# K, V and the gate logit in the spare columns of the last FFN chunk, and one written list of steps for the whole main phase

## The chip, the cores and the metric

The kernel runs on one core of a Trainium2 chip. The metric is device microseconds of that core, from the first to the last instruction and what lies around them; the median of the runs counts.

## The reference, cut to what matters

```python
B, S, D, H = 1, 2048, 512, 32          # Dh = 16; one K and one V head for all 32 query heads
q = x @ wq ; k = x @ wk ; v = x @ wv   # k and v are 2048 x 16
a = softmax(q k^T / 4) v, heads side by side, @ wo
b = (gelu(x @ w_gate) * (x @ w_up)) @ w_down      # F = 1376, tanh form of gelu
g = sigmoid(sum(x * gate_w))
out = g * a + (1 - g) * b
```

Everything is float32. The kernel makes most products in three passes: each factor is split into a high part (its rounded value, hi) and a low part (the rest, lo), and hi·hi, hi·lo and lo·hi are added in PSUM.

## The kernel before, in words

The 2048 tokens are four groups of 512 (TG). The 1376 hidden columns of the FFN are eleven chunks of 128 (NF), so that the last chunk has 1376 − 10·128 = 96 real columns and 32 of zeros.

**Prologue** (lines 291 to 322). The groups come in the order 1, 2, 3, 0. For each, TensorE (PE) makes `pk`, 12 products of 128x512 that give K (three times), V and the gate logit from a small weight tile `wkv` (L296), and then four blocks of Q, `pq`, of 12 products each (L301). `post_k` copies K into `kp` and V into `vt`; `post_q` splits a block of Q, takes its largest value for the softmax bound and writes it to DRAM (`scr`), from where it is read back in another layout as `Q`. Beside this ScalarE (ACT) and VectorE (DVE) split the next group of x. Behind the last block stand the 24 products of FFN chunk 0 of group 0 at full width (L509 to L518), with the bound's small steps `pairmax` and `shift_row` among them; then a branch on the bound (L528), of which the normal data take the short side.

**Main phase** (L564 on). Three kinds of work share PE, and a word of letters says how they are laced:

- S or Z: one score step, two products of 51 rows at once (L584), into one of three PSUM tiles of two banks: S takes tile 0 or 1 in turn, Z takes tile 2. ACT follows with one exponential of 128x1024 (L587). There are 1024 such steps.
- V: probabilities times V for one key chunk, four products onto four column strips (L657), in plain float32, which the trace shows as eight rows. There are 512 of them, 16 to a unit; behind a unit `norm` copies the sum out of PSUM, and the next unit uses the same bank. Here a run of V steps with other work ahead and behind is called a visit.
- F: a pair of products on the upper and the lower 64 rows of PE (L364), one for `z` and one for `y`, between H (the job's two PSUM banks are taken; z lies in tile 2) and R (the results go on to DVE). A gate job (an FFN chunk's gate and up product) and an output job (attention result times wo) have 24 pairs, a down job 18 or 12.

Behind a gate job's R, DVE copies z out (L389) and makes the gelu's inside (L392, L393), ACT the tanh, DVE the rest (L399, L400) and the two halves `hh` and `hl`. Weights arrive through `st` and are split by DVE (hi, L129) and GpSimd (lo, L130) in slots of the jobs. `WORDS` holds one word per kind of job (twelve for FFN and output jobs, one for the end). A V asks for a count, and `visit` (L667) decides how many steps are taken: never past a unit's end, at most four, the rest carried to the next visit. Output jobs come in as soon as a group's attention is ready.

**Tail**: norm of the last unit and the last output product.

Of the kernel before, what the change touches and what calls it, by code (L numbers as in the profile page):

```python
# [19 lines left out]
P = 128  # L20
# [12 lines left out]
QK = 51  # L33
SCALE = DH ** -0.5
# [7 lines left out]
WORDS = {  # L42
# [13 lines left out]
}  # L56
# [3 lines left out]
def mix_kernel(ctx, tc, xT, wq, wkv, wo, wf, out):  # L60
# [17 lines left out]
    shs = dr.tile([NTG * NB, 2, 3, 4, TG], F32, name="shs")  # L78

# [29 lines left out]
    wks = pp.tile([P, NC, P], F32, name="wks")  # L109
    wqs = p2.tile([P, NC, D], F32, tag="xr", name="wqs", bufs=4)  # L110
    xr = {tg: p2.tile([P, NC, TG], F32, tag="xr", name=f"xr{tg}", bufs=4) for tg in order[:3]}
    nc.scalar.dma_start(wks, wkv)
# [9 lines left out]
    load_x(order[1])  # L122
    load_x(order[2])
# [8 lines left out]
    wkh = pp.tile([P, NC, P], F32R, name="wkh")  # L132
    wkl = pp.tile([P, NC, P], F32R, name="wkl")
# [18 lines left out]
    split(nc.vector, nc.vector, wkh, wkl, wks)  # L152
    split_x(order[0], 0)
    split_x(order[0], 1)
    split_x(order[0], 2)
    split_x(order[0], 3)
# [27 lines left out]
    def post_k(tg, pk):  # L184
        sl = slice(tg * TG, (tg + 1) * TG)
        for r in (0, 64):
            nc.scalar.copy(kp[r : r + KR, sl], pk[0:KR])
        nc.scalar.copy(vt[32 * tg : 32 * tg + 32], pk[64:96])
        nc.vector.tensor_reduce(kmx[0:KR, tg : tg + 1], pk[0:KR], axis=AX, op=ALU.max, apply_absolute_value=True)
        for r in (32, 96):  # L190
            nc.vector.tensor_sub(kp[r : r + 16, sl], pk[32:48], kp[r : r + 16, sl])

    def post_v():
        pv = ps_a.tile([P, 4, P], F32, tag="pa", name="pv")
# [25 lines left out]
    chunks = [(tg, f) for tg in range(NTG) for f in range(NF)]  # L220
    W = {}
    stage = {}
# [6 lines left out]
    def fetch_w(n):  # L229
        if n < len(chunks):  # L230
            stage[n] = cp.tile([P, 3, D], F32, tag="st", name=f"st{n}", bufs=2)
            nc.sync.dma_start(stage[n], wf[chunks[n][1]].rearrange("p (t d) -> p t d", t=3))

    def split_w(n):
        if n not in stage:
            return []
        st = stage.pop(n)
        gh = cp.tile([P, 2, NC, P], F32R, tag="gh", name=f"gh{n}", bufs=2)
        gl = cp.tile([P, 2, NC, P], F32R, tag="gl", name=f"gl{n}", bufs=2)
        dh = cp.tile([P, D], F32R, tag="dh", name=f"dh{n}", bufs=4)  # L240
        dl = cp.tile([P, D], F32R, tag="dl", name=f"dl{n}", bufs=4)
        W[n] = gh, gl, dh, dl
        view = lambda t: st[:, t].rearrange("p (c f) -> p c f", c=NC)
        parts = [(gh[:, t], gl[:, t], view(t)) for t in range(2)] + [(dh, dl, st[:, 2])]
        return [lambda part=part: split(nc.vector, nc.gpsimd, *part) for part in parts]
# [45 lines left out]
    fetch_w(0)  # L291
    fetch_w(1)
    for ti, tg in enumerate(order):
        xh, xl = xs[tg]
        pk = ps_a.tile([P, TG], F32, tag="pa", name=f"pk{tg}")
        passes(pk, lambda c: wkh[:, c], lambda c: wkl[:, c], lambda c: xh[:, c], lambda c: xl[:, c], NC)  # L296
        post_k(tg, pk)
        for b in range(NB):
# [3 lines left out]
            if ti + 1 < NTG:  # L302
                split_x(order[ti + 1], b)
            post_q(tg, b, pq, ti == NTG - 1 and b == NB - 1)
            if ti == NTG - 1 and b == 0:
                for part in split_w(0):
                    part()
            if ti == NTG - 1 and b == 1:
                post_v()
            if ti == NTG - 1 and b == 2:  # L310
                load_q(0)
# [21 lines left out]
    wo_jobs = []  # L333
    hold = []
# [50 lines left out]
    def gelu(n, g, u):  # L385
# [16 lines left out]
        def halves():  # L402
            hh = cp.tile([P, TG], F32R, tag="hh", name=f"hh{n}", bufs=3)
            hl = cp.tile([P, TG], F32R, tag="hl", name=f"hl{n}", bufs=3)
# [12 lines left out]

    def gate_job(n):
        tg, f = chunks[n]

        def begin():
            flush(todo)
            if n == 1:
                fetch_w(2)
            fetch_w(n + 2)
            if n == 2:
                fetch_split("wo", wo, lambda: (woh, wol), lazy)
            defer(5 if n == 1 else 2, lambda: todo.extend(split_w(n + 1)))
            return weights_terms(n, 0), weights_terms(n, 1)

        def end(z, y):
# [4 lines left out]
            if f == NF - 1 and tg + 1 < NTG:  # L436
                reload_x(tg + 1)

        kind = "ABC"[f % 3] if f < NF - 2 else "ab"[f - NF + 2]
        return "L" if n == 1 else kind, begin, end  # L440

    def down_job(batch, i):
        tg, f = chunks[batch[0][0]]
# [6 lines left out]
        def begin():  # L450
            if f == 0 and i == 0:
# [3 lines left out]
        def end(z, y):  # L455
            for k, ps in ((i, z), (i + 1, y)):
                o = acc[tg][:, k]
                w = gc[:, 4 * tg + k : 4 * tg + k + 1]
                if f == 0:
# [4 lines left out]
        return ("DE" if len(batch) == 3 else "de")[i // 2], begin, end  # L464
# [10 lines left out]
    def wo_job(g, i):  # L475
        def begin():
            flush(lazy)
            return [[t for bl in range(NB) for t in wo_terms(g, k, bl)] for k in (i, i + 1)]
# [5 lines left out]
        return "WX"[i // 2], begin, end  # L484

    def jobs():
        for n, (tg, f) in enumerate(chunks):
            if n > 0:
                yield gate_job(n)
            if f % 3 == 2 or f == NF - 1:  # L490
                flush(chain)
                batch = hold[:]
                hold.clear()
                for i in (0, 2):
                    yield down_job(batch, i)
            while wo_jobs and wo_jobs[0][0] <= now[0]:
                g = wo_jobs.pop(0)[1]
                for i in (0, 2):
                    yield wo_job(g, i)
# [9 lines left out]
    ps = ps_f.tile([P, TG], F32, tag="pf", name="g0")  # L509
    terms = weights_terms(0, 0)  # L510
    chain_mm(ps, terms[:9], last=False)
    pairmax()
    chain_mm(ps, terms[9:], first=False)
    up0 = ps_a.tile([P, TG], F32, tag="pa", name="u0")
    terms = weights_terms(0, 1)
    chain_mm(up0, terms[:3], last=False)
    shift_row()
    chain_mm(up0, terms[3:], first=False)  # L518
    gelu(0, ps, lambda: up0)
    rest = split_w(1)  # L520
    for part in rest[:2]:
        part()
# [67 lines left out]
    def norm(u):  # L590
# [34 lines left out]
        def high(cs):  # L625
            if (g, b) not in O:
                assert not [j for j in wo_jobs if j[1] < g]
# [3 lines left out]
        def low(cs):  # L631
            oh, ol = O[g, b]
            nc.vector.tensor_sub(ol[:, cs], N[:, cs], oh[:, cs])  # L633
            if g < NTG - 1 and b == NB - 1:
                wo_jobs.append((now[0] + 4, g))
# [25 lines left out]
    at_s, at_v, carry = [0], [0], [0]  # L661
# [5 lines left out]
    def visit(k):  # L667
        if at_v[0] == nsteps:
            return
# [5 lines left out]
        if left - take == 1 and take < 3 and ready > take:  # L675
            take += 1
        carry[0] = want - take
        for _ in range(take):
            pv(at_v[0])
            at_v[0] += 1  # L680
        if take and at_v[0] % NKC == 0:
            if at_v[0] < nsteps:
                norm(at_v[0] // NKC - 1)

    def play(word, job=None):
        if job:
            X, Y = job[1]()
        for t in word.split():
# [14 lines left out]
            else:  # L703
                assert next(pairs, None) is None
                job[2](z, y)
# [6 lines left out]
    rest[2]()  # L712
# [4 lines left out]
    for job in jobs():  # L717
        play(WORDS[job[0]], job)
    while at_v[0] < nsteps:
        play(WORDS["T"])  # L720
# [16 lines left out]
_INS = ["xT", "wq", "wkv", "wo", "wf"]  # L737


def _layout(i):  # L740
# [7 lines left out]
    part = lambda w: w.reshape(NC, P, -1).transpose(1, 0, 2)  # L748
    pad = np.zeros((P, NC, 16), np.float32)
    wk = part(f("A_wk"))  # L750
    ins["wkv"] = np.concatenate([wk, wk, wk, pad, part(f("A_wv")), part(f("gate_w")), pad[:, :, 0:15], pad, pad], axis=2)
    ins["wo"] = f("A_wo").reshape(NB, 2, 4, DH, D).transpose(2, 1, 3, 0, 4).reshape(P, NB, D)

    def cols(w):
        w = np.pad(w, ((0, 0), (0, NF * P - F)))
# [3 lines left out]
    ins["wf"] = np.concatenate([cols(f("B_w_gate")), cols(f("B_w_up")), wd], axis=2)  # L759
# [18 lines left out]
```

## Time and profile before

| | |
|---|---|
| median of 3 runs | 1265.14 us (1263.65 to 1265.22) |
| the profiled execution | 1263.97 us |
| its span, first to last instruction | 1262.2 us |
| PE busy in the span | 1247.7 us |
| ACT busy | 1031.1 us |
| DVE busy | 574.8 us |
| first product of the prologue, first score step, last V step | 6.27, 72.80, 1245.0 us |

All times of single instructions are of the profiled execution, in which PE ran at a mean granted clock of 0.997. Products overlap on PE, so a row's own duration is longer than the time until the next one starts; what a product costs is read from the distance between starts.

### The profile page before, as it was taken

The page shows a single profiled execution, that of the slowest core. Times are in us where ns is not written, and L with a number is a line of the kernel's source. Part 1 is how long each engine was busy: PE and PEld are TensorE (multiplying, and loading weights), DVE is VectorE, ACT ScalarE, POOL GpSimd, SP SyncE. Part 2 cuts the span into 40 slices and gives each one's busy share as a digit, 9 for nine tenths or more (in the row PEclk, how much of TensorE's full clock was granted, in tenths as well). Part 3 has the DMA queues.
Part 4 walks back from the last instruction along what each step waited for, and adds up shares of the span by engine and source line. Part 5 has one row for each costly group of instructions (what it writes and reads, how often), then busy time and mean ns, then how long its engine had stood idle before and what let it go on. Part 6 is the DMA issues. An engine that isn't in the chain of part 4 may idle for free.

```text
span 1262.2 us, 23911 instructions
## 1 busy us (share of the span) xinstructions
PE 1247.7 (99%) x9886; PEld 667.8 (53%) x9886; DVE 574.8 (46%) x861; ACT 1031.1 (82%) x1118; POOL 222.6 (18%) x264
## 2 busy tenths in 40 slices
PE   9989999999999999999999999999999999999998
PEld 6855544554455555554555555554554555555554
DVE  6773352625553163443555145362546325354334
ACT  5358888888888888888888888888888888888883
POOL 3132211211220120212131012120232002112100
PEclk9999999999999999999999999999999999999999
DMA  8441111111210211111020021011111003101000
GB/s 316 166 155 56 44 39 47 39 39 56 81 40 14 70 54 39 64 40 56 28 93 1 31 81 64 26 53 39 51 53 59 15 31 106 39 27 39 14 1 35
DMA packets 26305, 72.63 MB, mean 58 GB/s; under 512 B 3984, under 2 KB 3984, under 8 KB 26192
## 3 DMA queue, kind: packets, MB, share of 16 engines
q1 hardware_dynamic: 25792, 70.01, 16.3%
q8 instruction: 79, 1.29, 0.4%
q0 software_dynamic: 256, 0.79, 0.2%
q14 instruction: 34, 0.28, 0.1%
q10 hardware_dynamic: 144, 0.26, 0.1%
HBM read 57.67 MB, written 13.37 MB: 56 GB/s over the span
## 4 chain that ended last, share of the span: by engine, by line
PE 90%; DVE 1%; ACT 1%; POOL 0%; issue 0%; DMA 0%; SPq 0%; ACTq 0%; DVEq 0%; POOLq 0%
PE acc L657 37%; PE s L584 22%; PE z L364 16%; PE y L364 14%; ACT p L587 1%; PE wos L349 1%; POOL gl L130 0%; DMA st<-wf 0%; DVE acc L472 0%; PE wof L349 0%; DVE sq L393 0%; DVE ol L633 0%; SPq L284 0%; DVE oh L629 0%; DVE dh L129 0%
## 5 line engine op out<-in xcount | busy, mean ns | idle before, releaser
L587 ACT ACTIVATE p<-s 128x1024 f32<-128x1024 f32 x1024 | 979.9, 1025 | 172.7 <-PE s L584 166.5
L657 PE MATMUL acc<-p,v 128*32 128x512 f32 x4096 | 490.9, 598 | 0.0
L584 PE MATMUL s<-Q,kp 51*128 51x512 f32 x2048 | 391.3, 419 | 5.2 <-SPq L528 2.7
L584 PEld LDWEIGHTS s<-Q,kp 51*128 51x128 f32 x2048 | 186.4, 184 | 247.4 <-ACT p L587 170.2
L657 PEld LDWEIGHTS acc<-p,v 128*32 128x32 f32 x4096 | 107.8, 109 | 247.0 <-issue 241.8
L130 POOL TENSOR_TENSOR gl<-st,gh 128x512 fp32r<-128x512 f32 x88 | 124.0, 1429 | 399.8 <-PE s L584 176.6
L389 DVE COPY gs<-z 128x512 f32<-128x512 f32 x43 | 29.7, 691 | 246.0 <-PE z L364 142.6
L364 PE MATMUL y<-xh,gh 64*128 64x512 f32 x344 | 138.6, 403 | 1.5 <-DVE gs L400 1.5
L364 PE MATMUL z<-xh,gh 64*128 64x512 f32 x344 | 138.4, 402 | 0.6 <-POOL mark L372 0.4
L364 PE MATMUL z<-xl,gh 64*128 64x512 f32 x344 | 134.9, 392 | 0.0
L364 PE MATMUL y<-xl,gh 64*128 64x512 f32 x344 | 134.9, 392 | 0.0
L364 PE MATMUL y<-xh,gl 64*128 64x512 f32 x344 | 134.8, 392 | 0.0
L364 PE MATMUL z<-xh,gl 64*128 64x512 f32 x344 | 134.8, 392 | 0.0
L372 POOL MEMSET mark<- 1x1 f32 x81 | 8.7, 108 | 583.3 <-PE y L364 579.2
L462 DVE SCALAR_TENSOR_TENSOR acc<-z,gc,acc 128x512 f32<-128x512 f32 x24 | 18.0, 751 | 146.8 <-PE z L364 125.1
L364 PEld LDWEIGHTS z<-xh,gh 64*128 64x128 f32 x344 | 64.3, 187 | 16.9 <-POOL mark L372 8.9
L364 PEld LDWEIGHTS z<-xh,gl 64*128 64x128 f32 x344 | 63.8, 186 | 9.7
L364 PE MATMUL z<-dh,hl 64*128 64x512 f32 x176 | 68.9, 391 | 0.0
L364 PE MATMUL y<-dh,hl 64*128 64x512 f32 x176 | 68.8, 391 | 0.0
L364 PE MATMUL z<-dh,hh 64*128 64x512 f32 x176 | 68.8, 391 | 0.0
L364 PE MATMUL z<-dl,hh 64*128 64x512 f32 x176 | 68.7, 390 | 0.0
L364 PE MATMUL y<-dh,hh 64*128 64x512 f32 x176 | 68.7, 390 | 0.0
(152 smaller groups left out, 1581.4 us busy)
## 6 DMA issues: line engine op xcount, KB each, us to landing
st<-wf SPq DMA_DIRECT2D x44, 768.0 KB
scr<-q SPq DMA_DIRECT2D x16, 512.0 KB
Q<-scr SPq DMA_DIRECT2D x64, 128.0 KB
Q<-scr SPq DMA_DIRECT2D x64, 64.0 KB
out<-acc SPq DMA_DIRECT2D x16, 256.0 KB
xr<-xT SPq DMA_DIRECT2D x6, 512.0 KB
xst<-xT SPq DMA_DIRECT2D x12, 256.0 KB
xr<-xT SPq DMA_DIRECT2D x4, 256.0 KB
```

The lines of the kernel that those rows point to most:

```text
L130: eng_l.tensor_sub(lo, src, hi)
L349: nc.tensor.matmul(ps, a, b, start=(first and q == 0), stop=(last and q == len(terms) - 1), skip_group_check=True)
L364: mm = nc.tensor.matmul(ps, a[rs], b[rs], start=(half == 0 and q == 0), stop=(half == 1 and q == len(X) - 1), skip_group_check=True)
L372: relay = nc.gpsimd.memset(mark, 0.0).ins
L389: nc.vector.tensor_copy(gs, g)
L462: nc.vector.scalar_tensor_tensor(o, ps, w, o, op0=ALU.mult, op1=ALU.add)
L584: nc.tensor.matmul(ps[:, j * TG : (j + 1) * TG], kp[rs, kc * P : (kc + 1) * P], Q[u][rs, pr], start=True, stop=True)
L587: nc.scalar.activation(p, ps, AF.Exp, bias=0.0, scale=SCALE)
L657: nc.tensor.matmul(accp[u][32 * j : 32 * j + 32], vt[:, kc], pb[s, j // 2][:, (j % 2) * TG : (j % 2 + 1) * TG], start=(kc == 0), stop=(kc ...
```

## The change

**Columns.** The separate weight tile for K, V and the logit is gone. In the last FFN chunk, K's 16 columns stand twice behind the 96 gate columns, and V's 16 and the logit's one behind the 96 up columns. The two products of this chunk, `gf` and `uf` (12 of 128x512 each), are made in the prologue for all four groups, in the place of `pk`. Rows 96 to 127 of them are K and V; rows 0 to 95 go through gelu in the prologue (`first_gelu`), on ACT, DVE and GpSimd, and the resulting halves of groups 1 to 3 are written to DRAM (`hs`) and read back when the group's turn comes (`reload_h`). So chunk 0 of each group in the new numbering (r = 0) is the last FFN chunk, and has no gate job. The next chunk's gate and up products of group 0 are the 24 full-width products in front of the branch. The splits of its weights and of the one after it move into the prologue's groups.

**List.** In place of words and `visit`'s rules there is a list of 78 words, one for each job in order (`f` FFN, `w` output, `t` the end). A V's count is taken as it stands.

```diff
-        pk = ps_a.tile([P, TG], F32, tag="pa", name=f"pk{tg}")
-        passes(pk, lambda c: wkh[:, c], lambda c: wkl[:, c], lambda c: xh[:, c], lambda c: xl[:, c], NC)
-        post_k(tg, pk)
+        last = ti == NTG - 1
+        first[tg] = [ps_f.tile([P, TG], F32, tag="pf", name=f"gf{tg}"), ps_a.tile([P, TG], F32, tag="pa", name=f"uf{tg}")]
+        for c in range(NC):
+            for t in range(1 if last else 2):
+                first_passes(tg, t, c)
+        post_k(tg, first[tg][0])
+        steps = first_gelu(tg)
+        steps[0]()
...
-            if ti == NTG - 1 and b == 0:
-                for part in split_w(0):
-                    part()
+            if b == 0:
+                steps[1]()
+            if b >= 1 and not last:
+                steps[b + 1]() if b < 3 else None
+            if ti == 0 and b == 3:
+                split_w(0)[0]()
+            if ti == 1 and b < 3:
+                if b == 0:
+                    parts = split_w(1)
+                parts[b]()
+                if b == 2:
+                    fetch_w(2)
...
+def first_gelu(tg):            # rows 0 to 95, lo = slice(0, 96)
+            nc.scalar.copy(gs[lo], g[lo])
+            nc.vector.scalar_tensor_tensor(sq[lo], gs[lo], GC, gs[lo], op0=ALU.mult, op1=ALU.mult)
+            nc.vector.scalar_tensor_tensor(sq[lo], sq[lo], 1.0, gs[lo], op0=ALU.add, op1=ALU.mult)
...
+            nc.scalar.activation(sq[lo], sq[lo], AF.Tanh, bias=0.0, scale=GS)
+            nc.vector.scalar_tensor_tensor(sq[lo], sq[lo], 1.0, gs[lo], op0=ALU.add, op1=ALU.mult)
...
+            nc.vector.scalar_tensor_tensor(gs[lo], u[lo], 0.5, sq[lo], op0=ALU.mult, op1=ALU.mult)
...
+            for h in (hh, hl):
+                nc.gpsimd.memset(h[RF:P].bitcast(F32), 0.0)
+            nc.scalar.copy(hh[lo], gs[lo])
+            nc.gpsimd.tensor_sub(hl[lo], gs[lo], hh[lo])
...
+                    nc.sync.dma_start(hs[tg - 1, a], h.bitcast(F32))
...
-    "C": "S Z S V3 Z S2 V H V S F3 S F3 S F6 S2 F6 S F6 R S2 V2 Z S2 V2",
...
+    "f: S V Z S2 V3 S Z S V2 S H F4 S F2 S F3 S V2 S F3 S F4 S F2 R",
...
     def visit(k):
-        want = k + carry[0]
-        left = NKC - at_v[0] % NKC
-        ready = at_s[0] // 2 - at_v[0]
-        take = max(min(want, left, ready, 4), 0)
...
-        for _ in range(take):
+        for _ in range(k):
             pv(at_v[0])
```

How rows move on PE at the start of the second group of the prologue; in a row, the result stands left of the arrow, and `xh`, `xl` are the group's halves of x, `wkh`, `gh` weights. Before:

```order
L181 MATMUL pq_3_279<-xh_142,wql 128x512
L181 MATMUL pq_3_279<-xl_143,wqh 128x512
L181 MATMUL pk_299<-xh_230,wkh 128x512
L181 MATMUL pk_299<-xh_230,wkl 128x512
L181 MATMUL pk_299<-xl_231,wkh 128x512
```

The same place of PE now:

```order
L251 MATMUL pq_3_311<-xh_145,wql 128x512
L251 MATMUL pq_3_311<-xl_146,wqh 128x512
L374 MATMUL gf_335<-xh_251,gh_117 128x512
L374 MATMUL gf_335<-xh_251,gl_118 128x512
L374 MATMUL gf_335<-xl_252,gh_117 128x512
L374 MATMUL uf_336<-xh_251,gh_117 128x512
L374 MATMUL uf_336<-xh_251,gl_118 128x512
L374 MATMUL uf_336<-xl_252,gh_117 128x512
```

Where 12 products of `pk` stood (three for each of four row chunks of x), 24 stand, `gf` and `uf` by turns.

What follows on PE in the main phase behind the last gate job of the first group's second batch; `s` is a score step (x4 is two of them), `acc` a V visit (x4 is one step). Before:

```order
L364 MATMUL z<-xh_432,gl_2572 128x512
L364 MATMUL y<-xh_432,gl_2572 128x512
L584 MATMUL s<-Q_2268,kp 128x512 x4
L657 MATMUL acc_2734<-p,v_74 32x512 x8
L584 MATMUL s<-Q_2268,kp 128x512 x6
L657 MATMUL acc_2734<-p,v_74 32x512 x12
L584 MATMUL s<-Q_2268,kp 128x512 x2
L364 MATMUL z<-dh_1958,hh_2608 128x512
```

The same place now:

```order
L503 MATMUL z<-xh_527,gl_2513 128x512
L503 MATMUL y<-xh_527,gl_2513 128x512
L738 MATMUL s<-Q_2387,kp 128x512 x2
L808 MATMUL acc_2816<-p,v_75 32x512 x4
L738 MATMUL s<-Q_2387,kp 128x512 x6
L808 MATMUL acc_2816<-p,v_75 32x512 x12
L738 MATMUL s<-Q_2387,kp 128x512 x6
L808 MATMUL acc_2816<-p,v_75 32x512 x8
L738 MATMUL s<-Q_2387,kp 128x512 x2
L503 MATMUL z<-dh_1879,hh_2545 128x512
```

Two visits of two and three steps have become three of one, three and two, and the first score step that uses tile 2 stands behind one V step and not behind two.

DVE in the second group of the prologue, between the second and the third block of Q (`xl` is the next group's low half, `qmx` and `q` belong to `post_q`). Before:

```order
L217 TENSOR_TENSOR q_1_355<-pq_1_340,q_1_355 128x512
L130 TENSOR_TENSOR xl_332<-xr_102,xh_331 128x512
L208 TENSOR_REDUCE qmx<-pq_2_360 128x1
L217 TENSOR_TENSOR q_2_375<-pq_2_360,q_2_375 128x512
L130 TENSOR_TENSOR xl_332<-xr_102,xh_331 128x512
```

The same engine and group now, from the first block's `q` to the third block's `xl`; `sqf`, `gsf` are the gelu's tiles and `gh` is a high half of weights:

```order
L286 TENSOR_TENSOR q_0_389<-pq_0_372,q_0_389 128x512
L390 SCALAR_TENSOR_TENSOR sqf_367<-sqf_367,gsf_366 96x512
L200 CAST gh_398<-st_199 128x512
L201 TENSOR_TENSOR xl_386<-xr_102,xh_385 128x512
L277 TENSOR_REDUCE qmx<-pq_1_402 128x1
L286 TENSOR_TENSOR q_1_417<-pq_1_402,q_1_417 128x512
L393 SCALAR_TENSOR_TENSOR gsf_366<-uf_336,sqf_367 96x512
L200 CAST gh_398<-st_199 128x512
L201 TENSOR_TENSOR xl_386<-xr_102,xh_385 128x512
```

Between two blocks of Q, a step of the gelu and a weight split have come in ahead of the next group's `xl`.

More of the change, by code (lines that the diff above doesn't have):

```diff
@@ L150, in split_x @@
         split(nc.scalar, nc.vector, xs[tg][0][:, c], xs[tg][1][:, c], xr[tg][:, c])
[L152 to L156, printed above, removed]
+    for t in range(2):
+        split(nc.vector, nc.vector, gh0[:, t], gl0[:, t], st0[:, t].rearrange("p (c f) -> p c f", c=NC))
+        for c in (2 * t, 2 * t + 1):
+            split_x(order[0], c)
     for c in range(NC):
@@ L218, in post_q @@
         nc.sync.dma_start(scr[i].rearrange("(t d) h q -> (d h) t q", t=2), q2.bitcast(F32))
-    chunks = [(tg, f) for tg in range(NTG) for f in range(NF)]
+    chunks = [(tg, r) for tg in range(NTG) for r in range(NF)]
     W = {}
-    stage = {}
+    stage = {0: st0}
     now = [-1]
@@ L435, in end @@
                 defer(k, advance(m))
[L436 to L440, printed above, removed]
+            if r == NF - 1:
+                flush(todo)
+                fetch_w(n + 3)
+                if tg + 1 < NTG:
+                    reload_x(tg + 1)
+        return begin, end
     def down_job(batch, i):
-        tg, f = chunks[batch[0][0]]
+        tg, r = chunks[batch[0][0]]
         def terms(k):
@@ L482, in end, with ffn_jobs @@
             wo_out(g, i + 1, y)
[L484 to L488, printed above, removed]
+        return begin, end
+    def ffn_jobs():
+        for n, (tg, r) in enumerate(chunks):
+            if r and n > 1:
                 yield gate_job(n)
-            if f % 3 == 2 or f == NF - 1:
+            if r % 3 == 2 or r == NF - 1:
                 flush(chain)
@@ L493, in jobs, with wo_jobs @@
                 hold.clear()
+                if r == NF - 1 and tg + 1 < NTG:
+                    reload_h(tg + 1)
                 for i in (0, 2):
                     yield down_job(batch, i)
[L496 to L499, printed above, removed]
+    def wo_jobs():
+        for g in range(NTG - 1):
+            for i in (0, 2):
+                yield wo_job(g, i)
     nsteps = 8 * NTG * NKC
@@ L507, in run_later @@
                     fn()
[L509 to L516, printed above, removed]
-    shift_row()
[L518 to L522, printed above, removed]
+    for c in range(NC):
+        first_passes(0, 1, c)
+        if c == 2:
+            pairmax()
+    v_rows(0)
+    for step in steps[2:]:
+        step()
+    ps = ps_f.tile([P, TG], F32, tag="pf", name="g1")
+    terms = weights_terms(1, 0)
+    chain_mm(ps, terms[:6], last=False)
+    shift_row()
+    chain_mm(ps, terms[6:], first=False)
+    post_v()
+    up1 = ps_a.tile([P, TG], F32, tag="pa", name="u1")
+    chain_mm(up1, weights_terms(1, 1))
+    gelu(1, ps, lambda: up1)
     pro.close()
@@ L716, in mix_kernel @@
         defer(k, advance(m))
[L717 to L720, printed above, removed]
+    queues = {"f": ffn_jobs(), "w": wo_jobs()}
+    for line in PLAN:
+        kind, word = line.split(":")
+        play(word, next(queues[kind]) if kind in queues else None)
+    assert at_v[0] == nsteps and not any(next(q, None) for q in queues.values())
     flush(chain)
```

157 lines of the change are left out of this document (97 added, 60 removed), and 89 rows, old and new, of tables (PLAN, WORDS).

## Prediction

> **What bounds the kernel now.** I read the busy times first, then the chain of work that ended last, then the main phase as one window.
>
> ```profile
> PE 1247.7 (99%) x9886; PEld 667.8 (53%) x9886; DVE 574.8 (46%) x861; ACT 1031.1 (82%) x1118; POOL 222.6 (18%) x264
> PE 90%; DVE 1%; ACT 1%; POOL 0%; issue 0%; DMA 0%; SPq 0%; ACTq 0%; DVEq 0%; POOLq 0%
> 100.00:1245.00 1145.00, 1141.88 (x9362) 590.33 (x9354) 494.34 (x731) 980.64 (x1045) 190.90 (x213) 1.00 0.14 45
> ```
>
> In the window's row, behind its length, stand the busy times of PE, weight loads, DVE, ACT and POOL. PE misses 3.1 us of 1145, at full clock, and carries 90% of the chain. ACT has 164 us to spare there. So time follows PE's list: products taken out shorten the kernel by what they cost, and anything that makes PE change its kind of work lengthens it. A busy PE need not be a PE at its best, so the prices are distances between starts. First full-width products, at three heads of prologue groups:
>
> ```profile
> 21.68 0.40 PE L181 MATMUL pk<-xh,wkh 128*128 128x512 f32 x1
> 35.69 0.39 PE L181 MATMUL pk<-xh,wkh 128*128 128x512 f32 x1
> 49.31 0.40 PE L181 MATMUL pk<-xh,wkh 128*128 128x512 f32 x1
> ```
>
> A group is 60 products: 14.01 and 13.62 us, so 0.230 us each on average. Then the main phase's kinds:
>
> ```profile
> 1235.24 0.40 PE L584 MATMUL s<-Q,kp 51*128 51x512 f32 x2
> 1235.47 0.39 PE L364 MATMUL z<-dh,hh 64*128 64x512 f32 x1
> ...
> 1236.17 0.40 PE L584 MATMUL s<-Q,kp 51*128 51x512 f32 x2
> 1236.50 1.07 PE L657 MATMUL acc<-p,v 128*32 128x512 f32 x8
> 1237.49 0.50 PE L584 MATMUL s<-Q,kp 51*128 51x512 f32 x2
> 1237.83 0.39 PE L364 MATMUL y<-dh,hh 64*128 64x512 f32 x1
> ```
>
> ```profile
> 1229.60 1.92 PE L657 MATMUL acc<-p,v 128*32 128x512 f32 x16
> 1231.45 0.73 PE L584 MATMUL s<-Q,kp 51*128 51x512 f32 x4
> ```
>
> Three pairs F take 0.70 us (1235.47 to 1236.17), 0.233 each; a score step between pairs 0.23. One V step takes 0.99, two take 1.85, so a step is 0.86 and a **visit** has a fixed price: 0.13 in the V rows (0.99 − 0.86), 0.10 in the score step ahead (0.33 against 0.23) and 0.11 in the one behind (0.34 against 0.23): 0.34 us.
>
> **The change part by part.**
>
> *Products.* Counted in PE's order, the full-width products up front rise from 264 (240 for K, V, Q and 24 of chunk 0) to 312 (192, 96 and 24): 48 × 0.230 = +11.0 us. The half-height products of the main phase fall from 3408 to 3216, by 96 pairs: 96 × 0.233 = −22.4 us. Score and V steps stay 1024 and 512. Sum **−11.4**, known to 0.2 (0.227 or 0.2335 for 0.230).
>
> *The list.* V runs in PE's order: 248 before (54 of one step, 125 of two, 68 of three, 1 of four), 268 after (108, 84, 68, 8). Twenty more visits: 20 × 0.34 = **+6.8**. But 31 visits now end straight on a pair and 20 start straight behind one, where the trace has three of the first and none of the second. Behind one of the three:
>
> ```profile
> 302.25 0.49 PE L364 MATMUL z<-xh,gh 64*128 64x512 f32 x1
> ...
> 302.81 0.40 PE L584 MATMUL s<-Q,kp 51*128 51x512 f32 x2
> ```
>
> The two pairs take 0.56 instead of 0.47: the same 0.10 that a score step pays. I take it for all joins; if all 51 direct joins were free it would be 5.1 less, at twice the price 5.1 more. [...]
>
> *Stalls of the main phase.* What PE waits for today is small:
>
> ```profile
> PE s L584 <- SPq L528: 2.7, 1, 2.7
> PE s L584 <- ACT p L587: 2.4, 6, 1.3
> PE y L364 <- DVE gs L400: 1.5, 1, 1.5
> ```
>
> (total, times, longest). The 2.7 is the branch and stays. The list leaves more between a gate job's R and the next H (at least 4.4 us of PE work against 3.0 before), and has 2 instead of 12 of 31 unit changes with only three score steps between them. I take **−1.0** for the last two rows, bounds −4 (all 3.9 gone) and +6 (a tenth of a microsecond at 60 of the 77 job ends; see the second rival).
>
> *Start.* The first products wait for the weight split:
>
> ```profile
> 4.97 0.80 DVE L129 CAST wkh<-wks 128x512 fp32r<-128x512 f32 x1 [3.80 <-DMA wks<-wkv]
> 5.80 0.69 DVE L130 TENSOR_TENSOR wkl<-wks,wkh 128x512 fp32r<-128x512 f32 x1
> 6.41 1.89 DVE L130 TENSOR_TENSOR xl<-xr,xh 128x512 fp32r<-128x512 f32 x3
> ```
>
> ```profile
> 6.27 0.58 PE L181 MATMUL pk<-xh,wkh 128*128 128x512 f32 x1
> ...
> 10.88 0.50 PE L181 MATMUL pq<-xh,wql 128*128 128x512 f32 x1 [0.23 <-DVE wql L130]
> ```
>
> Before, 13 products took 4.61 us (6.27 to 10.88), 1.6 over their price. Now DVE splits `gh0` (to 6.5), two chunks of x at 0.63 (to 7.7), and only then the up half, 1.5 us (to 9.2), while PE has spent its three `gf` products by 7.0. From 9.2, 20 products of 0.23 end at 13.8, where 24 at their price from 6.27 would end at 11.8: 2.0 over. The weights of Q are then long split. **+0.5**, bounds 0 and +1.6 (as much again as is lost today, for the first load is 256 KB larger).
>
> *Gelu, splits and copies in the prologue.* A group gives PE 72 × 0.230 = 16.6 us. DVE, by these rows:
>
> ```profile
> L130 DVE TENSOR_TENSOR xl<-xr,xh 128x512 fp32r<-128x512 f32 x16 | 10.8, 683 | 0.6 <-ACT xh L127 0.5
> ```
>
> ```profile
> 157.10 0.69 DVE L389 COPY gs<-z 128x512 f32<-128x512 f32 x1 [0.26 <-PE y L364]
> 157.83 0.69 DVE L392 SCALAR_TENSOR_TENSOR sq<-gs 128x512 f32<-128x512 f32 x1
> ```
>
> ```profile
> 58.05 2.84 POOL L130 TENSOR_TENSOR gl<-st,gh 128x512 fp32r<-128x512 f32 x2 [44.38 <-DVE gh L129]
> 58.21 1.52 DVE L129 CAST dh<-st 128x512 fp32r<-128x512 f32 x1
> 59.65 0.68 DVE L208 TENSOR_REDUCE qmx<-pq 128x1 f32<-128x512 f32 x1
> ```
>
> ```profile
> 70.38 2.77 POOL L130 TENSOR_TENSOR gl<-st,gh 128x512 fp32r<-128x512 f32 x2 [8.24 <-DVE gh L129]
> 71.95 1.75 DVE L392 SCALAR_TENSOR_TENSOR sq<-gs 128x512 f32<-128x512 f32 x1
> ```
>
> Fifteen operations that the old groups had too at 0.68 (four `xl`, eight of `post_q`, three of `post_k`) are 10.2; four gelu operations at 0.69 are 2.8; three weight casts, of 512 elements like `gs`, at 0.4 to 0.69 are at most 2.1: at most 15.1 us, inside the 16.6. While POOL works (58.05 to 60.89, 70.38 to 73.15), a cast takes 1.52 and the gelu's product 1.75, but `qmx`, which reads PSUM, still 0.68. POOL gets 4.3 for a chunk's three low halves (half of 2.84 each) and some 2.4 for the gelu's (one more, and two fills), ACT four short steps, the SP queue 1.5 MB to `hs`; all lie beside products. I take **+0.5**, bounds 0 and +12 (first rival). Later, a `reload_h` of 512 KB stands on SP three times, two down and two gate jobs ahead of its use, in a phase whose DMA share is 0.14 (window's row): nothing, and at most three times this load of 768 KB:
>
> ```profile
> 76.13 4.36 DMA st<-wf
> ```
>
> *Behind the last block of Q* stand 36 products instead of 24 (counted above), with the bound's steps between; PE reaches the branch later than DVE's last copy for it, so I add nothing.
>
> Sum: −11.4 + 6.8 − 1.0 + 0.5 + 0.5 = −4.6. From the profiled execution's 1263.97 that is 1259.4; the median of the runs lies 1.2 above that execution, so the forecast is **1260.6**.
>
> **The rivals.**
>
> 1. *DVE falls behind in the prologue* (slower or no gain). If POOL slows all casts and two-input products of groups 2 and 3 as in the rows above, they take 3 × 1.5 + 4 × 1.75 + 4 × 1.5 for `xl` = 17.5 in the place of at most 7.6 (2.1, 2.8, 2.7), and a group 25 us of DVE against 16.6 of PE. POOL is busy 6.7 of 16.6 us, 40%, so likelier 15.1 + 0.4 × 9.9 = 19.1 at most: two groups put DVE up to 5 us behind. PE feels it when `xl`'s last chunk is later than the 18 products (4.1 us) that come ahead of it; that is the point from which it decides. [...] At 40% some 0.5 to 1 us is lost, the half microsecond taken; if POOL's work falls wholly on DVE's, 2 × 8.4 − 4.1, some 12 us, and the time is 1272. Chance 0.1.
>
> 2. *Tile 2 comes free too late* (slower). Now 31 of 77 job ends have at most one score and one V step between R and the next Z; before, none of 81. z must be copied out first (157.10 above), behind an R at 156.91:
>
> ```profile
> 156.91 0.62 PE L584 MATMUL s<-Q,kp 51*128 51x512 f32 x4
> ```
>
> ```profile
> DVE gs L389 <- PE z L364: 142.6, 24, 13.8
> DVE gs L389 <- PE y L364: 103.4, 18, 13.8
> L620 DVE RECIPROCAL nz<-n 128x128 f32<-128x128 f32 x60 | 54.0, 928 | 0.5
> ```
>
> The copy ends 0.88 behind R; score and V step take 0.33 + 1.0, so Z has 0.45 to spare. DVE sat idle before 42 of the 43 copies, so it is usually ready. If it were in one of its 0.9 us reciprocals each time, Z would be 0.5 late, 31 × 0.5 = 15 us: 1276. It decides from some 15 such ends, 7 us: 1268. Chance 0.1.
>
> 3. *Visits cost less where pairs join them* (faster still): 5.1 less, 1255.5. For it: nothing in the trace but the absence of such joins. Chance 0.12.
>
> 4. *The gain goes into small waits*: the bounds of start and stalls add up to 3 to 6 us, 1263 to 1266. Chance 0.2.
>
> **How the numbers follow.** The forecast, 1258 to 1262.6, has 0.48; rival 3 has 0.12, rival 4 0.2, rivals 1 and 2 0.1 each. The range 1254 to 1267 takes in rival 3 below and rival 4 above and leaves out the two others' full prices. A measurement of this kernel tells 0.2% (2.5 us) from no change. Faster by more, under 1262.6: forecast and rival 3, 0.6, and a little of rival 4: 0.62. Within: 0.24. Slower, over 1267.7: 0.14, from rivals 1 and 2.
>
> **What would show each step.** Right: some 22 us fewer between first score step and last V step for the pairs, 7 of them given back; first score step near 84.8 (72.8 + 11.0 + 0.5 + 0.5); pairs behind a visit at 0.56 for two. Wrong: PE rows in the prologue waiting on `xl` (rival 1); Z's score steps waiting on L528's copy, the new line of the gelu's z copy (rival 2); a direct join at 0.47 (rival 3); more than 4 us of waits of score steps on ACT's exponentials. A main phase in which ACT is busy to over 95% of a window would overturn the reading that PE bounds it.

## The result and the profile after

The changed kernel takes **1301.4 us** (median of four runs, 1297.8 to 1304.0), the kernel before 1265.2 (1263.7 to 1265.9): 1.0286 times the time of before, 95% interval 1.0256 to 1.0316. The forecast was 1260.6, the range ended at 1267. The page's busy times, its chain by engine, and the main phase as one window (columns as in the prediction: PE, weight loads, DVE, ACT, POOL, clock, DMA share, GB/s):

```profile
PE 1260.4 (97%) x9742; PEld 653.5 (50%) x9742; DVE 559.7 (43%) x843; ACT 1033.5 (79%) x1126; POOL 222.9 (17%) x264
PE 88%; DVE 4%; ACT 1%; issue 1%; DMA 0%; ACTq 0%; SPq 0%; DVEq 0%
```

```profile
100.00:1245.00 1145.00, 1115.72 (x8946) 557.34 (x8938) 467.69 (x686) 951.65 (x1014) 185.65 (x203) 0.99 0.14 44
```

PE now misses 29.3 us of the 1145 instead of 3.1, and DVE has 4% of the chain instead of 1%. PE has fewer products (x9742 against x9886) and yet more busy time, 1260.4 against 1247.7 us: some of them took longer, and the clock of 0.99 hints at why. So three questions: what PE waits for, why DVE is in the chain, and where the clock went. First the waits (total, times, longest):

```profile
ACT p L741 <- PE s L738: 169.4, 239, 2.8
PE s L738 <- ACT p L741: 25.6, 16, 1.9
ACT sq L535 <- DVE sq L532: 24.8, 15, 1.9
PE y L503 <- DVE gs L539: 7.1, 5, 1.7
```

Score steps wait 25.6 us for exponentials (2.4 before), and the first y product of a job 7.1 us for the gelu's last product (1.5 before). The row between them is the lead: ACT's tanh (L535) waits 24.8 us in 15 waits for DVE's inside of the gelu (L532). ACT is busy 79% of the span and yet late, since it stands still at the head of its queue. One of these places, ACT, DVE and PE together, behind an R whose last products start at 169.16:

```profile
168.19 1.94 ACT L741 ACTIVATE p<-s 128x1024 f32<-128x1024 f32 x2
171.77 0.63 ACT L535 ACTIVATE sq<-sq 128x512 f32<-128x512 f32 x1 [1.64 <-DVE sq L532]
172.30 1.92 ACT L741 ACTIVATE p<-s 128x1024 f32<-128x1024 f32 x2
```

```profile
169.37 0.41 PE L738 MATMUL s<-Q,kp 51*128 51x512 f32 x2
169.59 0.69 DVE L528 COPY gs<-z 128x512 f32<-128x512 f32 x1 [2.47 <-PE z L503]
169.72 1.06 PE L808 MATMUL acc<-p,v 128*32 128x512 f32 x8
170.32 0.69 DVE L531 SCALAR_TENSOR_TENSOR sq<-gs 128x512 f32<-128x512 f32 x1
170.71 0.73 PE L738 MATMUL s<-Q,kp 51*128 51x512 f32 x4
171.04 0.69 DVE L532 SCALAR_TENSOR_TENSOR sq<-sq,gs 128x512 f32<-128x512 f32 x1
173.36 0.50 PE L738 MATMUL s<-Q,kp 51*128 51x512 f32 x2 [1.92 <-ACT p L741]
```

At 170.13 ACT ends the last exponential ahead of the tanh and then idles 1.64 us, although the scores of 169.37 lie ready: the tanh stands in front of their exponential and waits for DVE, which needs three steps of 0.7 us behind R. PE makes three score steps, which fill its three tiles, and waits 1.92 us for the first of them to be emptied. DVE is not late here: it sat idle for 2.47 us before its copy. It is the tanh that is early. In the trace of before, at the same kind of place (S2 V Z S and one more score step, R's scores at 156.91 as quoted in the prediction):

```profile
157.41 1.94 ACT L587 ACTIVATE p<-s 128x1024 f32<-128x1024 f32 x2 [0.59 <-PE s L584]
159.28 0.63 ACT L396 ACTIVATE sq<-sq 128x512 f32<-128x512 f32 x1
159.82 2.83 ACT L587 ACTIVATE p<-s 128x1024 f32<-128x1024 f32 x3
```

Here two exponentials stand ahead of the tanh, and when they are done its input is ready.

**Why the tanh moved.** A gate job's end puts the tanh off to the third score step to come (`defer(3, …)`). But the generator that hands out the jobs contains these lines (the kernel before has `f` for `r`) ahead of the two down jobs of a batch, because their products read the gelu's halves. `flush(chain)` issues all that is left of the gelu at once:

```python
            if r % 3 == 2 or r == NF - 1:
                flush(chain)
                batch = hold[:]
                ...
```

They run when the next job is asked for. In the old words the batch's last gate job goes on behind R (`R S2 V2 Z S2 V2`), so the job after it is asked for five score steps later. In the list every word ends with R, and the steps that stood behind it now begin the next word (`S V S Z S V3 …`): the job is asked for, and the chain emptied, right behind R, ahead of those steps. For the 16 gate jobs that end a batch the tanh so moves two exponentials forward, though no line on the gelu was touched.

**The clock.** In the main phase the granted clock falls to 0.50 in stretches of 3.41 us. In windows of that length, one around such a wait, the next one, and one around the wait shown above:

```profile
246.79:250.20 3.41, 1.49 (x14) 0.48 (x6) 2.54 (x5) 1.80 (x3) 0.00 (x0) 1.00 0.00 0
250.20:253.61 3.41, 3.41 (x18) 0.79 (x20) 3.34 (x6) 2.48 (x3) 0.00 (x0) 0.50 0.00 0
171.70:175.11 3.41, 1.75 (x15) 0.61 (x19) 2.54 (x6) 3.34 (x5) 0.00 (x0) 1.00 0.00 0
```

Behind the first, in which PE works 1.49 of 3.41 us, the granted clock is 0.50 for 3.41 us; behind the last, with 1.75, it stays at 1.00. Seven stretches of half clock lie in the main phase, from 96.60, 250.20, 564.23, 683.70, 799.75, 888.50 and 1117.19 on (to the nearest hundredth). Each costs half its length, 1.7 us: three V steps across the fifth take 4.41 us (798.81 to 803.22), at full clock 2.71 (173.79 to 176.50). The seven make 12 us in all, which is most of PE's extra busy time. All seven follow a window with a score step's wait of about 1.9 us; at five further places with a wait as long, the one at 173.36 among them, the wait lies across two windows, with at most 1.66 us in one of them, and the clock stays.

**The waits on y** have another cause: something stands ahead of the gelu's last products in DVE's queue. DVE, ACT's tanh and PE's y product at one of the five places:

```profile
761.61 0.62 ACT L535 ACTIVATE sq<-sq 128x512 f32<-128x512 f32 x1
764.68 0.69 DVE L762 COPY n<-acc 128x512 f32<-128x512 f32 x1 [3.60 <-PE acc L808]
765.29 0.68 DVE L538 SCALAR_TENSOR_TENSOR sq<-sq,gs 128x512 f32<-128x512 f32 x1
766.00 0.69 DVE L539 SCALAR_TENSOR_TENSOR gs<-y,sq 128x512 f32<-128x512 f32 x1
766.75 0.49 PE L503 MATMUL y<-xh,gh 64*128 64x512 f32 x1 [1.48 <-DVE gs L539]
```

The tanh is done at 762.2, but the gelu's next product (L538) starts at 765.29: in DVE's queue `norm`'s copy of the finished unit stands ahead of it and waits 3.60 us for the visit's last V step. The copy has moved ahead of it since the visit that ends the unit now lies between the third and the fifth score step behind R.

### The profile page after: what moved, and what is told of

The parts are those of the page before. It is cut to its first block, busy times and chain, and to the rows that moved or that the text cites. A ratio compares the mean times of both kernels' runs of the same rounds, so it can differ in the third digit from the quotient of the medians.

```text
span 1301.3 us, 23608 instructions
## 1 busy us (share of the span) xinstructions
PE 1260.4 (97%) x9742; PEld 653.5 (50%) x9742; DVE 559.7 (43%) x843; ACT 1033.5 (79%) x1126; POOL 222.9 (17%) x264
## 3 DMA queue, kind: packets, MB, share of 16 engines
q8 instruction: 77, 1.26, 0.4%
## 4 chain that ended last, share of the span: by engine, by line
PE 88%; DVE 4%; ACT 1%; issue 1%; DMA 0%; ACTq 0%; SPq 0%; DVEq 0%
PE acc L808 36%; PE s L738 22%; PE z L503 16%; PE y L503 14%; ACT p L741 1%; DVE sq L531 1%; DVE sq L532 1%; DVE gs L528 1%; PE wos L488 1%; DVE gs L539 0%; DVE sq L538 0%; DMA Q<-scr 0%; DVE acc L620 0%; DVE nz L774 0%; ACT sq L535 0%
## 5 line engine op out<-in xcount | busy, mean ns | idle before, releaser
L808 PE MATMUL acc<-p,v 128*32 128x512 f32 x4096 | 505.8, 610 | 0.0
L738 PE MATMUL s<-Q,kp 51*128 51x512 f32 x2048 | 408.7, 426 | 27.1 <-ACT p L741 25.6
L503 PE MATMUL y<-xh,gh 64*128 64x512 f32 x312 | 123.5, 396 | 5.5 <-DVE gs L539 5.4
L503 PE MATMUL z<-xh,gh 64*128 64x512 f32 x312 | 123.0, 394 | 0.3 <-ACT p L741 0.3
L503 PE MATMUL z<-xl,gh 64*128 64x512 f32 x312 | 122.3, 392 | 0.0
L503 PE MATMUL y<-xl,gh 64*128 64x512 f32 x312 | 122.1, 391 | 0.0
L503 PE MATMUL z<-xh,gl 64*128 64x512 f32 x312 | 122.0, 391 | 0.0
L503 PE MATMUL y<-xh,gl 64*128 64x512 f32 x312 | 121.9, 391 | 0.0
L503 PE MATMUL y<-dl,hh 64*128 64x512 f32 x176 | 68.8, 391 | 0.0
L201 POOL TENSOR_TENSOR dl<-st,dh 128x512 fp32r<-128x512 f32 x44 | 58.3, 1325 | 54.2 <-DVE dh L200 51.9
```

What stands on the lines that cost most here:

```text
L201: eng_l.tensor_sub(lo, src, hi)
L503: mm = nc.tensor.matmul(ps, a[rs], b[rs], start=(half == 0 and q == 0), stop=(half == 1 and q == len(X) - 1), skip_group_check=True)
L738: nc.tensor.matmul(ps[:, j * TG : (j + 1) * TG], kp[rs, kc * P : (kc + 1) * P], Q[u][rs, pr], start=True, stop=True)
L808: nc.tensor.matmul(accp[u][32 * j : 32 * j + 32], vt[:, kc], pb[s, j // 2][:, (j % 2) * TG : (j % 2 + 1) * TG], start=(kc == 0), stop=(kc ...
```

## The experiments

Theory 1 is that the early tanh holds up ACT's queue, and that the stalls, where they fill half of a 3.41 us window, cost the clock as well. Its rivals are that DVE is too slow wherever the tanh stands (theory 2), that visits and direct joins are dearer than priced (theory 3), and, in one run, that the new columns by themselves bring the loss. Every kernel was timed against the kernel before, whose median was 1264.9 beside the first four of these runs, 1264.8 beside the next four and 1265.7 beside the last.

### The tanh back behind two exponentials: late_flush

A down job collects its inputs, and empties the chain, at its H. `batch` is now handed over empty and filled by the down job's `begin`, which `play` calls there; the reload of the first chunk's halves moves with it.

```diff
-                flush(chain)
-                batch = hold[:]
-                hold.clear()
+                batch = []
...
             elif t[0] == "H":
                 advance(1)()
+                if late:
+                    X, Y = job[0]()
```

> The changed kernel, but a down job collects its inputs (and so empties the gelu's chain) at its H and not at the start of its word; the tanh of the 16 gate jobs that end a batch then stands behind two more exponentials on ACT. Theory 1 (the early tanh holds ACT's queue up): 14 waits of score steps on exponentials go, 12 x 1.9 + 1.3 + 1.0 = 25 us, and with them the seven stretches of 3.4 us at half clock, 7 x 1.7 = 12 us: 1301.4 - 37 = 1264, 1260 to 1269, half clock nowhere in the main phase. Theory 2 (DVE delivers the gelu's inside too late wherever the tanh stands): the waits move and stay, 1290 to 1302. Theory 3 (visits and direct joins cost more than priced, the waits are the smaller part): the waits go, but 1275 or more remains.

Measured: 1269.4 us, 1.0033 times before (1.0022 to 1.0043): 32 us of the 36 are gone, though it ends just above the range of 1260 to 1269, and two stretches at half clock are left in the main phase where I expected none. Of the waits of score steps on exponentials one of 0.3 us is left. What remains is a row of the other kind:

```profile
PE y L503 <- DVE gs L539: 10.5, 8, 1.7
```

It has grown from 7.1 to 10.5 us: in two down jobs the gelu's last product, formerly issued early together with the tanh, now lies behind `norm`'s copy too, and both waits (1.71 and 1.26 us) are followed by a stretch at half clock (from 307.70 and 925.51). Without these, 2 × 1.7 + 1.71 + 1.26 = 6.4 us, it would be 1263. The theory of a slow DVE (1290 and more) and that of dear visits (1275 and more) fall. The edit moves the whole chain, DVE's products with the tanh; that the tanh is what PE felt is read from the rows above, where DVE idles and ACT's exponential stands behind the tanh.

### The gelu's product ahead of norm's copy: late_flush_outer

late_flush, and besides, in `visit`:

```diff
             if at_v[0] % NKC == 0 and at_v[0] < nsteps:
+                if len(chain) == 2:
+                    advance(1)()
                 norm(at_v[0] // NKC - 1)
```

> As late_flush, and besides, where a visit ends a unit, the gelu's last two products are put into DVE's queue ahead of norm's copy. Theory 1 extended: the five waits of H's first y product on the gelu's last product (1.24 + 1.24 + 1.48 + 1.47 + 1.65 = 7.1 us) come from the copy that stands ahead of it and waits for the end of the V visit; they go: 7 us under late_flush, 1257, 1253 to 1262. If those waits come from a job head that is too short for the gelu in any order, it is the same as late_flush within 2 us.

Measured: 1257.2 us, 0.9936 times before (0.9924 to 0.9949), 0.6% less than the kernel before. The gain over late_flush is 12.2 us: 8.4 us of waits on y and two stretches at half clock (3.4 us). One of the five waits that I expected to go, 1.64 us at the head of an output job, is still there; late_output_jobs below takes it up. That the time falls on the forecast of 1257 is partly luck: late_flush was 5 us above its own, and this gain 5 us larger than the 7 forecast. Its page and its main phase:

```profile
PE 1244.6 (99%) x9742; PEld 651.1 (52%) x9742; DVE 558.8 (45%) x843; ACT 1034.3 (82%) x1126; POOL 222.7 (18%) x264
```

```profile
100.00:1245.00 1145.00, 1141.83 (x9250) 576.38 (x9247) 480.76 (x710) 983.39 (x1047) 185.56 (x206) 1.00 0.14 44
```

PE's busy time is 15.8 us less than in the changed kernel with the same 9742 products, of which 12 us were clock, and it misses 3.2 us of the window, as before the change. At the place where the wait on y stood, the gelu's product now runs beside the V steps and the copy behind it:

```profile
733.69 0.62 ACT L535 ACTIVATE sq<-sq 128x512 f32<-128x512 f32 x1
734.34 0.69 DVE L538 SCALAR_TENSOR_TENSOR sq<-sq,gs 128x512 f32<-128x512 f32 x1 [1.18 <-ACT sq L535]
735.13 0.69 DVE L539 SCALAR_TENSOR_TENSOR gs<-y,sq 128x512 f32<-128x512 f32 x1
736.75 0.69 DVE L767 COPY n<-acc 128x512 f32<-128x512 f32 x1 [0.92 <-PE acc L813]
```

### The same fault in the kernel before: before_early_flush

The kernel before, with one thing changed: the chain is emptied right behind R of a batch's last gate job (at the end of `gate_job`'s `end`).

```diff
+            if f % 3 == 2 or f == NF - 1:
+                flush(chain)
```

> The kernel before, with the gelu's chain emptied right behind R of each gate job that ends a batch, the rest as it was. Theory 1: the same loss appears in the old list without any other part of the change: ACT idles some 1.6 us behind the exponentials in flight, and PE waits 1.1 us (two V steps in the head) to 2.0 us (one) at some 12 to 16 places: 1265 + 14 to 30, and half clock only behind stalls near 1.9 us, so 1279 to 1300. Theories 2 and 3: the place of the tanh matters little, 1265 to 1270.

Measured: 1297.5 us, 1.0258 times before (1.0231 to 1.0285): 33 us lost, against 36 for the whole change. Neither columns nor list are in it.

```profile
ACT sq L396 <- DVE sq L393: 36.0, 18, 2.8
PE s L586 <- ACT p L589: 21.6, 33, 1.8
PE y L364 <- DVE gs L400: 1.5, 1, 1.5
```

The waits on exponentials are back, in pairs of 1.07 and 0.42 us at most places, since the old words take two V steps there; and in the main phase the clock falls to a half four times, from 91.94, 388.9, 699.5 and 1013.5 on. Of the 34.4 us between the two profiled executions (spans 1296.6 − 1262.2) these waits make 19.2, the four stretches 6.8, and a longer half clock at the branch (6.8 us against 3.4) 1.7; the other 7 are not traced further. I had expected half clock only behind stalls near 1.9 us; of the four windows ahead of these stretches three hold 1.50 us without PE. So the length of a single stall does not decide alone.

### A shorter stall: short_inside

The changed kernel without its second step of the gelu's inside:

```diff
             nc.vector.scalar_tensor_tensor(sq, gs, GC, gs, op0=ALU.mult, op1=ALU.mult)
-            nc.vector.scalar_tensor_tensor(sq, sq, 1.0, gs, op0=ALU.add, op1=ALU.mult)
```

> The changed kernel with one of the two products of the gelu's inside left out (the cubic term's second factor is missing, so the gelu is another function). Theory 1: each of the 14 hold-ups gets 0.7 us shorter, 14 x 0.7 = 10 us; at 1.2 us no window of 3.4 us is half idle any more, so the seven stretches at half clock go too, 12 us: 1279, 1275 to 1284. If the half clock is no cost of its own (or is not set off by the length of the stall): 1288 to 1293. Theory 2: more than 10 us also comes from the other gate jobs, with waits left where they were. Theory 3: about 1300.

Measured: 1281.4 us, 1.0124 times before (1.0107 to 1.0141), 20.0 less than the changed kernel.

```profile
PE s L737 <- ACT p L740: 15.3, 15, 1.3
ACT sq L534 <- DVE sq L531: 14.0, 15, 1.2
PE y L503 <- DVE gs L538: 6.4, 5, 1.5
```

The waits themselves are only 11.0 us shorter (25.6 + 7.1 − 15.3 − 6.4). The other 9 us are the clock: none of the seven stretches at half clock is left, and one new one has come (from 754.05, behind a wait of 1.48 us on y that the changed kernel has without it), so 6 × 1.7 = 10.2 us less. So the half clock is a cost of its own, near what the rows give. That it went with the shorter stalls and came with those of before_early_flush shows that the stalls set it off.

### The price of a visit: more_visits

late_flush_outer with 17 visits more, by 17 edits of the list like this:

```diff
-    "f: S V S Z S V3 S Z S V2 H F S F3 …",
+    "f: S V S Z V S V2 S Z S V2 H F S F3 …",
```

> late_flush_outer with 17 more visits: at 17 places of the list one V step of three is taken one score step earlier (S V3 S becomes V S V2 S); nothing else changes. If a visit has the fixed price that the prediction took from the rows of before, 0.34 us: 17 x 0.34 = 5.8, so 1257.2 + 5.8 = 1263.0, 1262 to 1264.5. If the price lies in the work beside it and not in the change of kind: 1257 to 1258.5. If a visit costs 0.6 (which would make visits a large part of the loss of the changed kernel): 1267.4.

Measured: 1264.1 us, 0.9992 times before (0.9982 to 1.0002), 7.0 above late_flush_outer. The median is raised by runs with a granted clock of 0.998 or 0.999, five of ten here and one of six there; between the two profiled executions, both at 1.00 in the main phase, it is 5.9 (spans 1261.3 − 1255.4), 0.35 for a visit. The price of 0.34 that the prediction read from distances between rows stands; the third theory falls here once more.

### The price of a direct join: more_direct_joins

late_flush_outer with 40 times `V S F3` made `V F S F2` (or the like).

> late_flush_outer with 40 more visits that end straight on a pair: behind them one pair is taken ahead of the score step (V S F3 becomes V F S F2); number of visits and all products as before. Price equal to that of a score step, as the prediction took it: 1257.2 within 1.5. Direct joins free (its third rival): 40 x 0.11 = 4.4 less, 1252.8. At twice the price: 4.4 more, 1261.6.

Measured: 1264.3 us, 0.9992 times before (0.9983 to 1.0002), 7.2 more than late_flush_outer. None of the three answers: of the 7.8 us between the two spans, 1.7 are a stretch at half clock behind the one wait of 1.68 us that late_flush_outer has too (1.64 there, without half clock), and the rest comes in steps of 0.2 to 0.25 us at some 26 places. But not at the joins: behind a visit one pair ahead of a score step takes 0.34 us, and a score step ahead of pairs takes 0.34. The time goes some steps later:

```profile
237.74 3.77 ACT L746 ACTIVATE p<-s 128x1024 f32<-128x1024 f32 x4 [0.63 <-PE s L743]
```

```profile
239.40 0.39 PE L503 MATMUL y<-xl,gh 64*128 64x512 f32 x1
...
239.74 0.19 PEld L743 LDWEIGHTS s<-Q,kp 51*128 51x128 f32 x2 [0.38 <-ACT p L746]
239.74 0.50 PE L743 MATMUL s<-Q,kp 51*128 51x512 f32 x2
240.08 0.39 PE L503 MATMUL y<-xh,gl 64*128 64x512 f32 x1
```

With a pair ahead of it the score step behind the visit starts later, ACT idles 0.63 us instead of 0.41, and its row of four exponentials ends later. The score step at 239.74 then gets its tile late, its weights are loaded only at 239.74 too (those of the score step at 237.25 already at 237.02), and the pair ahead of it (239.40 to 239.74) and the step itself (239.74 to 240.08) take 0.34 us each instead of 0.23. So the join's price is that of the prediction, but the edit was not clean: at this place it also took work from ACT just where ACT had run dry.

### The columns alone: columns_old_words

The new columns with words, `play` and `visit` of before.

> The new columns with the words and visit rules of before (no list; its word tails stand behind R again). The products up front are those of the changed kernel, the main phase has its 96 pairs fewer, and 264 visits; as the old words run out, 28 rounds of two score steps and a V step stand at the end with no products beside them, where two exponentials (1.93 us) take longer than PE's 1.55: 28 x 0.4 = 11 us. Theory 1: no waits of 1.9 us, since no chain is emptied early: 1264.9 - 11.4 + 16 x 0.34 + 11 - 1.7 (no half clock behind the branch) = 1268, 1263 to 1273. If the new columns by themselves bring the loss (prologue, DVE, reload of the halves): 1285 or more.

Measured: 1271.0 us, 1.0051 times before (1.0034 to 1.0067), inside the range of the sum.

```profile
PE s L676 <- ACT p L679: 7.4, 21, 0.9
PE y L438 <- DVE gs L474: 2.5, 1, 2.5
```

Score steps wait 7.4 us, mostly in the rounds at the end, none of them over 0.9; one y product waits 2.5 us for the gelu (at 96.53), and there is no half clock in the trace. The columns don't bring the loss, but with the old words they bring no gain either.

### Two steps further: late_output_jobs and score_step_first

late_output_jobs is late_flush_outer with `begin.late` for output jobs too, so that `norm`'s remaining steps (reciprocals and products that stood ahead of the gelu's last ones there) no longer enter DVE's queue at the word's start.

> late_flush_outer, with the output jobs too collecting their inputs at H, so that norm's remaining steps no longer go into DVE's queue ahead of the gelu's last product at the word's start. The 1.64 us in which the first y product of an output job waits for that product should go: 1255.5, 1254.5 to 1257. If the wait comes from the shortness of the job's head: 1257.2.

Measured: 1255.3 us, 0.9924 times before (0.9908 to 0.9941): the 1.64 us are gone. score_step_first is late_output_jobs with eleven times `V F S F2` made `V S F3`.

> late_output_jobs with 11 direct joins in the middle of a word taken back (V F S F2 becomes V S F3). If a score step behind a visit keeps ACT fed, as more_direct_joins showed in 26 of its 40 places (0.23 us each), the mirror edit gains where ACT is late there: 0 to 2.5 us less than 1255.3. If those joins were placed where ACT has room: 1255.3 within 0.6.

Measured: **1254.4 us**, 0.9918 times before (0.9902 to 0.9935), 0.9 less than late_output_jobs: inside the first answer (0 to 2.5 less), just outside the second (within 0.6). So a few of those joins seem to have starved ACT; the effect is small. It is the fastest kernel of the study, 47 us under the changed one.

## Why the prediction was wrong

The failed step is *Stalls of the main phase*, "I take −1.0 …, bounds −4 … and +6". It measured +29 us (25.6 of score steps behind the early tanh and 7.1 of y products behind DVE's queue, against 3.9 before) and took 12 us of half clock with it, for which the sum had no term at all. I argued from the distance between R and H and from the copy of z, neither of which lies in ACT's queue; rival 4 had waits, but bounded them by 3 to 6 us. That steps which stood behind an R now stand behind the fetch of the next job, and that this fetch empties the gelu's chain into ACT's queue, I did not look at, though the order of ACT's instructions shows it without a run. The prediction's own sign, "more than 4 us of waits of score steps on ACT's exponentials", is what appeared, with 25.6.

The other steps, by the rows. First the ends of the prologue (first score step) and of the main phase (first product of the tail), in the changed kernel and in late_flush_outer:

```profile
82.84 0.93 PE L738 MATMUL s<-Q,kp 51*128 51x512 f32 x4 [1.41 <-DMA Q<-scr]
...
1285.83 0.50 PE L488 MATMUL wos<-woh,oh 128*128 128x512 f32 x1
```

```profile
82.89 0.93 PE L743 MATMUL s<-Q,kp 51*128 51x512 f32 x4 [1.32 <-DMA Q<-scr]
...
1239.98 0.50 PE L488 MATMUL wos<-woh,oh 128*128 128x512 f32 x1
```

```profile
72.80 0.70 PE L584 MATMUL s<-Q,kp 51*128 51x512 f32 x2 [2.66 <-SPq L528]
...
1245.04 0.50 PE L349 MATMUL wos<-woh,oh 128*128 128x512 f32 x1
```

- **Products up front, start, DVE and POOL in the prologue: right in their sum.** PE ends its last product there at 81.43 instead of 70.14 (the score step's start less its wait), 11.3 us later against 12.0 forecast. No product there waits on `xl` for 0.15 us or more: rival 1 did not come.
- **The wait at the branch: missed, a little to the good.** I said that its 2.7 us stay. It is 1.4 us now, and the half clock from 74.0 to 77.4 in the trace of before, which I had not seen and which costs 1.7 us, is gone too:

```profile
74.00:75.00 1.00, 1.00 (x8) 1.00 (x7) 1.00 (x1) 0.61 (x1) 0.85 (x1) 0.50 0.61 199
```

- **Products and visits of the main phase: the prices right, the sum some 3 us too good.** It is 1203.0 us long in the changed kernel, 1172.2 before, and 1157.1 in late_flush_outer, which has the same steps on PE: 15.1 us less than before against 16.6 forecast. Of the 15.1, 1.7 are the half clock of before, which leaves 13.4 for the terms of the sum. A visit measured 0.35 (0.34 forecast), a direct join 0.34 for a pair (0.33 to 0.34 forecast), so rival 3 fell.
- **Rival 2, z's bank: did not come.** No score step waits on the copy of z: the two at 170.71, of which the first uses z's tile, start as the V step ends, and the row says nothing of a wait. The second rival had the right place, the few steps between R and what follows, and the wrong engine: the copy, from 169.59 for 0.69 us, has 0.43 us to spare, the tanh two more DVE steps behind it has none.

Of the 46 us between the main phases of the changed kernel and late_flush_outer, 30 are waits (33.0 against 3.0) and 12 clock. The other 4 show as no wait of PE, but by an estimate from starts they stand at the same places: at some 18 of them more than in late_flush_outer the step ahead of the wait takes 0.39 us beside it where 0.23 is usual, and the step behind it 0.43 (173.36 to 173.79) where 0.33 is usual, 18 × 0.26 = 4.7 us.

The forecast was 1260.6, and late_flush_outer, without the early tanh, has 1257.2. That they lie so near is in part luck. Its main phase gains 3 us less than the terms say; against that stand things for which the sum had nothing: 1.3 us at the branch, the 1.7 of half clock behind it, a tail that is 1.8 us shorter (15.4 us from its first product on against 17.2, not traced further), and 1.2 us by which the median of before lay above its profiled execution and that of late_flush_outer does not.

## What to carry to other kernels

When steps are regrouped, look at what runs at the seams, not only at the steps. In these traces a waiting instruction stood in its engine's queue where its issuing code was called, and what was queued behind it waited too: on ACT an exponential stood 1.64 us behind the tanh, on DVE the gelu's product from 762.2 to 765.29 behind `norm`'s copy. Compare the order of every engine's instructions around the seam, also of those with time to spare: ACT was busy 79% of the span, and its order cost most of the 36 us. And a stall of PE is not always paid by its length alone: here each of the nine that left PE idle for 1.71 us or more of a 3.41 us window cost 1.7 us more.

## What the hardware showed

**In these traces the clock followed PE's activity in fixed windows.** The seven starts of half clock in the changed kernel lie 45, 92, 35, 34, 26 and 67 times 3.413 us apart, to within 0.05 us, and each stretch lasts one such window, 3.41 us at a granted clock of 0.50. In the five traces of the changed kernel, late_flush, before_early_flush, short_inside and the kernel before, half clock followed every main-phase window that PE left idle for 1.71 us or more (nine), none with under 1.25, and five of the twelve from 1.25 to 1.66. What decides between these stays open.

**A score step behind a visit fed ACT.** In more_direct_joins one pair ahead of it cost about 0.2 us at some 26 of 40 places, not there but, at the place that was followed (ACT idle for 0.63 us instead of 0.41), where the exponentials it had delayed were next waited for.
